# Weight loads that cast on the way, a changed order of GpSimd's early work, fewer loads per pair, and a last tile in halves

## Chip, cores, metric

The kernel runs on one core of a Trainium2 chip. The metric is the device time of one execution in microseconds. One execution was also recorded by the hardware profiler. Engines are named as in the profile: PE (TensorE matmul), PEld (its weight load), DVE (VectorE), ACT (ScalarE), POOL (GpSimd), SP (SyncE, which here only issues DMAs).

## What is computed

Attention with a sliding window and a few "sink" keys, followed by a two-layer network with a gate:

```python
# q, k, v: (4, 8, 768, 64) float32; n_sink = 4, window = 128
scores = matmul(q, k^T) / sqrt(64)
keep = (key position < 4) | (0 <= query position - key position < 128)
a = softmax(where(keep, scores, -1e9))
attn = matmul(a, v)                          # (4, 8, 768, 64)
x = attn.transpose(0, 2, 1, 3).reshape(3072, 512)
h = x @ w_in                                 # w_in: 512 x 2048
g = h * sigmoid(beta * h)
out = g @ w_out                              # w_out: 2048 x 512, out float32
```

## The kernel before, in words

**Tiling.** Two heads that lie side by side make a pair, and half a sequence (384 tokens) of a pair is a *unit* `n`: 32 units, of which four in a row (`4T` to `4T + 3`) give one tile `T` of 384 tokens by 512 channels. There are 8 tiles. `place(n)` gives a unit's batch, pair, half and buffer. A unit goes through these steps:

1. `load` (L372): q, k and v come by DMA as float32 into `q_stage`, `k_stage`, `v_stage`. Units 0 to 11 come half by half, units from 16 on for both halves of a pair at once, one DMA for each head of q, k and v, so six DMAs a pair.
2. `cast` (L417): POOL makes bf16 of q, k (into `qk16`, three buffers) and v (into `v_aug`).
3. Transposes: units 0 to 11 by PE (`transpose_in`, L447), later ones by a transposing DMA on SP's queue (L432).
4. Scores on PE (L487, L521), exponentials on ACT (L493, L528), masks on DVE (L502, L537: a product of two bf16 tiles), the product with v on PE (`attend`, L571), for the second half of a sequence with the sink keys too (`v_sink`, L560), then the normalisation on DVE (L581) and the way back into `xT` (L598, or a transposing DMA, L590).

**The network.** For each tile 16 blocks of hidden channels: `hidden` (L618, four 128x384 matmuls each), the tanh on ACT (L626), the gate on DVE (L639), and `project` (L646, three blocks of 128 tokens, 16 matmuls of 512 columns each), whose result ACT or DVE scales by 0.5 into `out_sb` (L654, L658), from where SP's queue stores it (L661).

**Weights.** Both weight matrices come in eight pieces of 0.5 MB each: 0 to 7 are `w_in`, 8 to 15 are `w_out`. `load_w(i)` (L407) issues a plain DMA on SP's queue into one of eight float32 buffers `wst`, and `cast_w(i)` (L412) is a copy on POOL that makes bf16 of it. `hidden` reads `w_in`: pieces 0 and 1 from block 0 on, 2 and 3 from block 4 on, 4 to 7 from block 8 on.

**Order.** The program is a list of operations with what they read and write. `Prog.order` (L140) plays them through with estimated durations and fixes from it, before the kernel runs, in which order each engine gets its instructions; at each step the operation that can start first is taken, the earlier in the list on a tie. For DMAs it holds one time, `dma_free`, at which all DMAs together are done with what was issued. `Prog.emit` then puts in the waits on semaphores. So a changed estimate or a new dependence can change the order on each engine.

The main list: constants; the loads of units 0 to 3 (v of units 0 and 1 on ACT's queue, the rest on SP's), weight pieces 0 to 3, units 4 to 7, weight pieces 4 to 7; units 0 to 3 through all their steps (`enter`, then scores, masks, `attend`), the POOL casts of pieces 0 to 3 and two small POOL DMAs for `v_sink` (L689) in `enter(1)`; then a loop over steps `s`, where step `s` runs one block of `hidden`, and units 4 to 31 are worked into it by the table `FIRST`. At step `FIRST[5] + 2 = -2` pieces 4 to 7 are cast and the loads of pieces 8 to 15 and of units 8 to 15 are listed; at step 2 pieces 8 to 15 are cast; at step 16 POOL copies the masks into `mask_all` (L767, L771: six copies), which units from 12 on use. From step 32 on (`S_P0`) `project` runs beside `hidden`, with `w_out`; after the last gate only `project` is left.

The list order is not the order in time: an operation without open dependences can be taken before earlier listed ones that wait. The chain of `mask_all` copies is an example: listed at step 16, they run on POOL at 5.64 us.

## Time and profile before

| | us |
|---|---|
| median of three runs (lowest, highest) | 240.41 (239.73, 241.25) |
| the profiled execution, whole | 241.05 |
| its span from first to last instruction | 239.3 |
| POOL's 64 casts of q and k, and 32 of v (L425, L428) | 36.4 and 17.1 busy |
| POOL's 16 weight casts (L414), mean of one | 1.04 |
| POOL's two `v_sink` DMA issues (L689), first at 4.28 | 0.62 and 0.76 |
| DVE's masks of units 0 to 11 (L502), 24 | 0.55 to 1.20 each |
| `project`'s matmuls (L646) | 98.5 busy |
| `hidden`'s matmuls (L618), both kinds of bank | 80.1 and 20.2 busy |
| issue to landing, weight loads of `w_in`, median | 6.8 |
| issue to landing, output stores (256 KB), median | 2.7; the last ones 2.0 |
| last PE matmul ends | 236.13 |
| last copy to `out_sb` (L654) | 236.21 to 236.81 |

How to read it: busy time counts an engine's instructions without its waits. "DMA share" is the mean busy share of the core's 16 DMA engines; overlapping packets can bring it over 1. The granted TensorE clock is 1.00 throughout. POOL's last cast of q and k begins at 149.5 us.

### The profile page before, as it was taken

What the parts mean: (1) busy time and instruction counts of PE and PEld (TensorE: products, weight loads), DVE (VectorE), ACT (ScalarE), POOL (GpSimd) and SP (SyncE); (2) the same over time, 40 slices, a digit from 0 to 9 for tenths busy, and PEclk for the clock granted to TensorE, in tenths of its full rate; (3) what the DMA queues carried; (4) which work ended last, traced back from release to release, by engine and by line L of the source; (5) the groups of instructions that cost most, each with busy time, mean ns of one, the idle gap of its engine ahead of it and who ended that gap; (6) DMA issues with size and microseconds to landing.
All of it is one profiled execution on the core that took longest, in us unless ns stands there. A gap on an engine that the chain in (4) does not pass through costs nothing.

```text
span 239.3 us, 4359 instructions
## 1 busy us (share of the span) xinstructions
PE 217.9 (91%) x1677; PEld 118.2 (49%) x1677; DVE 137.7 (58%) x262; ACT 147.7 (62%) x254; POOL 73.3 (31%) x134
## 2 busy tenths in 40 slices
PE   0567769799999999999999999999999999999994
PEld 0244435455545555554555555555555555555441
DVE  4066499859974565653676537664666656434300
ACT  2477487559852756765877667658767865554411
POOL 7989568529251133232223337000000000000000
PEclk9999999999999999999999999999999999999999
DMA  7999999899799999999999976512201022111022
GB/s 176 260 374 280 334 377 294 221 284 251 169 227 207 209 183 276 231 164 216 225 167 237 195 148 152 126 28 60 63 16 47 16 60 63 44 44 44 5 85 88
DMA packets 96084, 39.76 MB, mean 166 GB/s; under 512 B 82736, under 2 KB 88896, under 8 KB 96064
## 3 DMA queue, kind: packets, MB, share of 16 engines
q1 hardware_dynamic: 93888, 39.07, 71.0%
q10 hardware_dynamic: 1632, 0.40, 0.8%
q8 instruction: 13, 0.21, 0.4%
q0 software_dynamic: 544, 0.02, 0.2%
q14 instruction: 7, 0.06, 0.1%
HBM read 27.30 MB, written 6.29 MB: 140 GB/s over the span
## 4 chain that ended last, share of the span: by engine, by line
PE 81%; DVE 11%; ACT 4%; POOL 2%; issue 1%; ACTq 0%
PE acc L646 34%; PE h_ps L618 28%; PE s_ps L571 5%; DVE E L502 5%; PE acc L618 4%; PE s_ps L521 4%; ACT E L493 2%; DVE g L639 2%; DVE qkT L454 1%; PE h_ps L646 1%; PE s_ps L487 1%; PE s_ps L560 1%; DVE v_sink L335 1%; PE s_ps L469 1%; DVE o_norm L581 1%
## 5 line engine op out<-in xcount | busy, mean ns | idle before, releaser
L646 PE MATMUL acc<-w_out,g 128*128 128x512 bf16 x368 | 98.5, 380 | 0.0
L626 ACT ACTIVATE th<-h_ps,beta_half 128x384 f32<-128x384 f32 x104 | 59.3, 582 | 39.0 <-PE h_ps L618 37.6
L618 PE MATMUL h_ps<-xT,w_in 128*128 128x384 bf16 x416 | 80.1, 326 | 0.2 <-DVE g L639 0.2
L639 DVE SCALAR_TENSOR_TENSOR g<-th,h_ps 128x384 bf16<-128x384 f32 x104 | 56.3, 552 | 33.3 <-ACT th L626 31.9
L618 PEld LDWEIGHTS h_ps<-xT,w_in 128*128 128x128 bf16 x416 | 39.6, 98 | 30.9 <-DVE g L639 1.7
L646 PEld LDWEIGHTS acc<-w_out,g 128*128 128x128 bf16 x368 | 34.4, 98 | 33.4 <-issue 3.0
L537 DVE TENSOR_TENSOR E<-E,mask_all 128x1536 bf16<-128x1536 bf16 x20 | 19.7, 984 | 26.4 <-ACT E L528 26.4
L528 ACT ACTIVATE E<-s_ps 128x1536 bf16<-128x1536 f32 x20 | 29.0, 1449 | 7.5 <-PE s_ps L521 7.1
L425 POOL CAST qk<-q_stage 128x384 bf16<-128x384 f32 x32 | 18.8, 588 | 34.2 <-DMA qkT<-qk 17.9
L428 POOL CAST v_aug<-v_stage 128x384 bf16<-128x384 f32 x32 | 17.1, 546 | 36.8 <-PE s_ps L571 35.9
L571 PE MATMUL s_ps<-v_aug,E 128*128 128x65 bf16 x384 | 21.1, 199 | 3.2 <-DVE E L502 3.0
L571 PEld LDWEIGHTS s_ps<-v_aug,E 128*128 128x128 bf16 x384 | 18.1, 101 | 9.0 <-DVE E L502 4.1
L618 PE MATMUL acc<-xT,w_in 128*128 128x384 bf16 x96 | 20.2, 341 | 1.6 <-DVE g L639 1.3
L654 ACT ACTIVATE out_sb<-acc 128x512 f32<-128x512 f32 x23 | 13.6, 597 | 11.3 <-PE acc L646 10.8
L581 DVE TENSOR_TENSOR o_norm<-s_ps,rden 128x384 bf16<-128x384 f32 x32 | 17.8, 558 | 1.8
L626 ACT ACTIVATE th<-acc,beta_half 128x384 f32<-128x384 f32 x24 | 13.8, 585 | 7.9 <-PE acc L618 7.4
L425 POOL CAST qk<-k_stage 128x384 bf16<-128x384 f32 x32 | 17.6, 550 | 0.1
L493 ACT ACTIVATE E<-s_ps 128x768 bf16<-128x768 f32 x16 | 13.0, 812 | 4.9 <-PE s_ps L487 4.7
L639 DVE SCALAR_TENSOR_TENSOR g<-th,acc 128x384 bf16<-128x384 f32 x24 | 13.0, 548 | 2.8 <-ACT th L626 2.7
L447 PE MATMUL s_ps<-ident,qk 128*128 128x128 bf16 x60 | 6.3, 246 | 8.8 <-POOL qk L425 8.3
L502 DVE TENSOR_TENSOR E<-E,mask_b 128x768 bf16<-128x768 bf16 x16 | 13.5, 847 | 1.2 <-ACT E L493 0.9
L618 PEld LDWEIGHTS acc<-xT,w_in 128*128 128x128 bf16 x96 | 8.4, 102 | 8.0 <-DVE g L639 3.5
(58 smaller groups left out, 147.4 us busy)
## 6 DMA issues: line engine op xcount, KB each, us to landing
out_dram<-out_sb SPq DMA_DIRECT2D x24, 256.0 KB, 2.7
q_stage<-in_q_dram SPq DMA_DIRECT2D x28, 192.0 KB, 4.3
k_stage<-in_k_dram SPq DMA_DIRECT2D x28, 192.0 KB, 4.9
wst<-in_moe_w_in_dram SPq DMA_DIRECT2D x8, 512.0 KB, 6.8
wst<-in_moe_w_out_dram SPq DMA_DIRECT2D x8, 512.0 KB, 7.6
v_stage<-in_v_dram SPq DMA_DIRECT2D x16, 192.0 KB, 4.0
v_stage<-in_v_dram SPq DMA_DIRECT2D x28, 96.0 KB, 5.0
q_stage<-in_q_dram SPq DMA_DIRECT2D x8, 96.0 KB, 4.1
```

The lines of the kernel that those rows point to most:

```text
L425: op("gp", lambda e, x=x, name=name: e.tensor_copy(qk16[z][:, x, :, :, :], view(name)), r=[(name + "_stage", pb, half, hh) for hh in range ...
L428: op("gp", lambda e: e.tensor_copy(v_aug[pb][:, 3 * half:3 * half + 3, :, 0:D], view("v")), r=[("v_stage", pb, half, hh) for hh in range(2 ...
L493: op("act", lambda e: e.activation(E[n % 2][:, c, :, 0:at], bank[:, 0:2, 0:at], AF.Exp, bias=0.0, scale=SCALE), x=[f"{name}0", f"{name}1"] ...
L502: op("dve", lambda e: e.tensor_tensor(E[n % 2][:, c, :, 0:w], E[n % 2][:, c, :, 0:w], m[:, first:first + w].unsqueeze(1).to_broadcast([128 ...
L528: op("act", lambda e: e.activation(E[z][:, :, :, :].rearrange("p c h x -> p c (h x)"), s_ps[:, :, :].rearrange("p (h b) x -> p h (b x)", h ...
L537: op("dve", lambda e: e.tensor_tensor(both, both, mask_all[:, half, :].unsqueeze(1).to_broadcast([128, 2, 768]), ALU.mult), r=[("E", z, 0) ...
L571: last=(x == len(kbs) - 1): e.matmul(av_ps[:, at + hh * D1:at + hh * D1 + D1], E[z][:, c, h2, col:col + 128], v_aug[pb][:, kb, hh, :], sta ...
L581: op("dve", lambda e: e.tensor_tensor(o_norm[o][:, :, :, :].rearrange("p m h d -> p (m h) d"), src[:, :, 0:D], rden[z][:, :].unsqueeze(2). ...
L618: op("pe", lambda e: e.matmul(bank, w_in16[:, c, m * 128:(m + 1) * 128], xT[:, c, T * TT:(T + 1) * TT], start=(c == 0), stop=(c == 3)), r= ...
L626: op("act", lambda e: e.activation(th[i % 3][:, :], bank, AF.Tanh, bias=0.0, scale=beta_half[:, m:m + 1]), x=[name], r=["beta"], w=[("th", ...
L639: op("dve", lambda e: e.scalar_tensor_tensor(g[T % 2][:, m, :], th[i % 3][:, :], 1.0, bank, ALU.add, ALU.mult), r=[("th", i % 3)], x=[name ...
L646: op("pe", lambda e: e.matmul(bank, g[T % 2][:, m, t * 128:(t + 1) * 128], w_out16[:, m, :], start=(m == 0), stop=(m == NM - 1)), r=[("g", ...
```

## The change

- **Weights**: `wst`, `w_piece` and `cast_w` go. `load_w` is now a DMA issued by POOL that reads float32 and writes bf16 straight into `w_in16` or `w_out16`. Each has a new kind of dependence, `after`: it waits until the cast of a given unit's v is done. Pieces 0 and 1 wait for unit 2, pieces 2 and 3 for unit 3, 4 and 5 for unit 4, 6 and 7 for unit 5, 8 to 11 for unit 6, 12 to 15 for unit 7.
- **POOL's early work**: the six copies to `mask_all` wait for the cast of unit 7; the two DMAs for `v_sink` wait for that of unit 4.
- **Loads**: units 8 to 11 wait for the cast of unit 5; they and units 12 to 15 are listed without weight pieces between them. From unit 16 on, q, k and v of a pair are one DMA each, for both heads and both halves: three DMAs for six.
- **The planner's picture of DMAs**: one time per issuing queue, with the rate shared between a queue and the one that is busy longest.
- **The last 128 tokens**: `project` for them is done in two halves of 256 columns, one after the other, into the two banks of `h_ps`. The first is scaled by DVE and stored by SP's queue, the second by ACT and stored by ACT's queue.

```diff
@@ -100,7 +101,8 @@
 
         return Together()
 
-    def op(self, eng, fn, r=(), w=(), x=(), dma=None, busy=100.0, lag=None, behind=None):
+    def op(self, eng, fn, r=(), w=(), x=(), dma=None, busy=100.0, lag=None, behind=None,
+           after=()):
         if self.group is not None and self.group.eng == eng:
             node = self.group
         else:
@@ -116,7 +118,7 @@
             if not same or (raw and eng != "pe"):
                 events.append(ev)
 
-        for t in r:
+        for t in (*r, *after):
             dep(self.writer.get(t), True)
         for t in (*w, *x):
             dep(self.writer.get(t), False)
@@ -148,7 +150,7 @@
         head = dict.fromkeys(self.ENGINES, 0)
         can = {e: [n for n in left[e] if n.open == 0] for e in self.ENGINES}
         placed = []
-        dma_free = self.FIRST_DMA
+        ring = dict.fromkeys(self.ENGINES, self.FIRST_DMA)
 
         def best(e):
             q = left[e]
@@ -171,8 +173,11 @@
                 n.done = start + n.busy + n.lag
             else:
 
-                dma_free = max(dma_free, start + n.busy) + n.lag
-                n.done = dma_free + 2000.0
+                at = max(ring[e], start + n.busy)
+                other = max(t for q, t in ring.items() if q != e)
+                shared = max(0.0, other - at)
+                ring[e] = at + (2 * n.lag if 2 * n.lag <= shared else n.lag + shared / 2)
+                n.done = ring[e] + 2000.0
             n.place = start
             can[e].remove(n)
             placed.append(n)
@@ -280,7 +285,6 @@
     xT = sb("xT", (128, 4, NTOK), BF16)
     w_in16 = sb("w_in16", (128, 4, DF), BF16)
     w_out16 = sb("w_out16", (128, NM, NOUT), BF16)
-    wst = [sb(f"wst{i}", (128, 1024), F32) for i in range(NW)]
     beta_stage = sb("beta_stage", (16, 128), F32)
     beta_half = sb("beta_half", (128, NM), F32)
     ones = sb("ones", (128, 256), BF16)
@@ -369,50 +373,50 @@
 
         return n // 8, n % 4, n // 4 % 2, n % 4
 
-    def load(n, v_queue="sp"):
+    def load(n, v_queue="sp", after=()):
         b, hp, half, pb = place(n)
         t0 = half * TT
         if n < XBAR:
             for name, src in (("q", q), ("k", k)):
                 s = src[b, 2 * hp:2 * hp + 2, t0:t0 + TT, :].rearrange("h (p c) d -> p h (c d)", c=3)
                 d = stage[name][pb][:, :, 3 * half:3 * half + 3, :].rearrange("p h c d -> p h (c d)")
-                op("sp", lambda e, d=d, s=s: e.dma_start(d, s),
+                op("sp", lambda e, d=d, s=s: e.dma_start(d, s), after=after,
                    w=[(name + "_stage", pb, half, 0), (name + "_stage", pb, half, 1)],
                    dma=f"{name}{pb}_{half}", **transfer(2 * TT * D * 4, 329))
-        halves = (0, 1) if n >= WHOLE else (half,)
-        first, size = (0, 6) if n >= WHOLE else (3 * half, 3)
         for name, src in (("q", q), ("k", k), ("v", v)):
+            if n >= WHOLE:
+                s = src[b, 2 * hp:2 * hp + 2, :, :].rearrange("h (c p) d -> p (h c) d", p=128)
+                d = stage[name][pb][:, :, :, :].rearrange("p h c d -> p (h c) d")
+                op("sp", lambda e, d=d, s=s: e.dma_start(d, s), after=after,
+                   w=[(name + "_stage", pb, x, hh) for x in range(2) for hh in range(2)],
+                   dma=f"{name}{pb}_0", **transfer(2 * S * D * 4, 220))
+                continue
             if name != "v" and n < XBAR:
                 continue
             for hh in range(2):
-                s = src[b, 2 * hp + hh, 128 * first:128 * (first + size), :].rearrange(
-                    "(c p) d -> p c d", p=128)
+                s = src[b, 2 * hp + hh, t0:t0 + TT, :].rearrange("(c p) d -> p c d", p=128)
                 op(v_queue, lambda e, hh=hh, s=s, name=name: e.dma_start(
-                    stage[name][pb][:, hh, first:first + size, :], s),
-                   w=[(name + "_stage", pb, x, hh) for x in halves],
-                   dma=f"{name}{pb}_{half}{hh}", **transfer(size * 128 * D * 4, 220))
+                    stage[name][pb][:, hh, 3 * half:3 * half + 3, :], s), after=after,
+                   w=[(name + "_stage", pb, half, hh)],
+                   dma=f"{name}{pb}_{half}{hh}", **transfer(TT * D * 4, 220))
 
     w_in_src = moe_w_in.rearrange("(c p) f -> p c f", p=128)
     w_out_src = moe_w_out.rearrange("(m p) n -> p m n", p=128)
 
-    def w_piece(i):
-        z = i % NW
+    def load_w(i, behind):
+
         if i < NW:
-            c, n = 2 * (z % 2), 512 * (z // 2)
-            view = wst[z][:, :].rearrange("p (c f) -> p c f", c=2)
-            return view, w_in_src[:, c:c + 2, n:n + 512], w_in16[:, c:c + 2, n:n + 512]
-        view = wst[z][:, :].rearrange("p (m n) -> p m n", m=2)
-        return view, w_out_src[:, 2 * z:2 * z + 2, :], w_out16[:, 2 * z:2 * z + 2, :]
-
-    def load_w(i):
-        view, src, _ = w_piece(i)
-        op("sp", lambda e: e.dma_start(view, src), w=[("wst", i % NW)], dma=f"w{i % NW}",
-           **transfer(1 << 19, 389))
-
-    def cast_w(i):
-        view, _, dst = w_piece(i)
-        op("gp", lambda e: e.tensor_copy(dst, view), r=[("wst", i % NW)],
-           w=[("w_in" if i < NW else "w_out", i % NW)], busy=985.0, lag=100.0)
+            c, n = 2 * (i % 2), 512 * (i // 2)
+            src, dst = w_in_src[:, c:c + 2, n:n + 512], w_in16[:, c:c + 2, n:n + 512]
+        else:
+            m = 2 * (i - NW)
+            src, dst = w_out_src[:, m:m + 2, :], w_out16[:, m:m + 2, :]
+        op("gp", lambda e: e.dma_start(dst, src), after=cast_of(behind),
+           w=[("w_in" if i < NW else "w_out", i % NW)], dma=f"w{i}", busy=710.0,
+           lag=(1 << 19) / 350.0)
+
+    def cast_of(n):
+        return [("v_aug", place(n)[3], place(n)[2])]
 
     def cast(n):
         _, _, half, pb = place(n)
@@ -642,24 +646,26 @@
 
     n_out = [0]
 
-    def project(T, t, m, bank, name, eng="act"):
-        op("pe", lambda e: e.matmul(bank, g[T % 2][:, m, t * 128:(t + 1) * 128],
-                                    w_out16[:, m, :], start=(m == 0), stop=(m == NM - 1)),
-           r=[("g", T % 2, m), ("w_out", m // 2)], w=[name], **pe(NOUT))
+    def project(T, t, m, bank, name, eng="act", cols=slice(0, NOUT), queue="sp"):
+        width = cols.stop - cols.start
+        op("pe", lambda e: e.matmul(bank[:, 0:width], g[T % 2][:, m, t * 128:(t + 1) * 128],
+                                    w_out16[:, m, cols], start=(m == 0), stop=(m == NM - 1)),
+           r=[("g", T % 2, m), ("w_out", m // 2)], w=[name], **pe(width))
         if m == NM - 1:
             z = n_out[0] % 4
             n_out[0] += 1
 
             if eng == "act":
-                op("act", lambda e: e.activation(out_sb[z][:, :], bank, AF.Copy, bias=0.0,
-                                                 scale=0.5),
-                   x=[name], w=[("out_sb", z)], **act(NOUT))
+                op("act", lambda e: e.activation(out_sb[z][:, 0:width], bank[:, 0:width], AF.Copy,
+                                                 bias=0.0, scale=0.5),
+                   x=[name], w=[("out_sb", z)], **act(width))
             else:
-                op("dve", lambda e: e.tensor_scalar(out_sb[z][:, :], bank, 0.5, None, ALU.mult),
-                   x=[name], w=[("out_sb", z)], **dve(600.0))
+                op("dve", lambda e: e.tensor_scalar(out_sb[z][:, 0:width], bank[:, 0:width], 0.5,
+                                                    None, ALU.mult),
+                   x=[name], w=[("out_sb", z)], **dve(1.17 * width))
             row = T * TT + t * 128
-            op("sp", lambda e: e.dma_start(out[row:row + 128, :], out_sb[z][:, :]),
-               r=[("out_sb", z)], dma=f"o{z}", **transfer(128 * NOUT * 4, 389))
+            op(queue, lambda e: e.dma_start(out[row:row + 128, cols], out_sb[z][:, 0:width]),
+               r=[("out_sb", z)], dma=f"o{z}", **transfer(128 * width * 4, 389))
 
 
     constants()
@@ -667,12 +673,8 @@
         load(n, "act" if n < 2 else "sp")
     op("act", lambda e: e.dma_start(beta_stage[:, :], moe_beta.rearrange("(m p) -> m p", p=128)),
        w=["beta_stage"], dma="beta")
-    for i in range(4):
-        load_w(i)
     for n in range(4, 8):
         load(n)
-    for i in range(4, 8):
-        load_w(i)
     cast(0)
     cast(1)
 
@@ -680,14 +682,16 @@
         transpose_in(n, *((tr_ps, "tr") if n % 2 == 0 else (acc[0], "acc0")), "act")
         if n + 2 < 6:
             cast(n + 2)
-        if n == 1:
-            for i in range(4):
-                cast_w(i)
+        if n < 2:
+            load_w(2 * n, n + 2)
+            load_w(2 * n + 1, n + 2)
+        if n == 3:
             for hh in range(2):
                 rows = slice(HEAD1 * hh, HEAD1 * hh + NSINK)
                 s = v[:, :, 0:NSINK, :].rearrange("b (g h) s d -> s h (b g) d", h=2)[:, hh]
                 op("gp", lambda e, hh=hh, rows=rows, s=s: e.dma_start(v_sink[rows, :, hh, 0:D], s),
-                   w=[("v_sink", hh)], r=["v_sink"], dma=f"s{hh}")
+                   w=[("v_sink", hh)], r=["v_sink"], after=cast_of(4), dma=f"s{hh}", busy=650.0,
+                   lag=700.0)
 
     for n in range(4):
         enter(n)
@@ -747,40 +751,28 @@
             cast(n)
             if n >= XBAR and n % 8 >= 4 and n + 4 < NU:
                 load(n + 4)
+        if s == FIRST[4]:
+            for x in range(4, 8):
+                load_w(x, 4 if x < 6 else 5)
         if s == FIRST[5] + 2:
-            for x in range(4, 8):
-                cast_w(x)
-            for x in (8, 9, 10, 11):
-                load_w(x)
-            load(8)
-            load_w(12)
-            load_w(13)
-            load(9)
-            load_w(14)
-            load_w(15)
-            for n in range(10, 16):
-                load(n)
+            for n in range(8, 16):
+                load(n, after=cast_of(5) if n < 12 else ())
         if s == NM:
 
             first = {0: (mask_a[:, :], MASK_A), 1: (mask_b[:, 128:512], MASK_B)}
             for half in range(2):
                 op("gp", lambda e, half=half: e.tensor_copy(mask_all[:, half, 0:TT], first[half][0]),
-                   r=first[half][1], w=[("mask_all", half, 0)], busy=300.0)
+                   r=first[half][1], after=cast_of(7), w=[("mask_all", half, 0)], busy=300.0)
                 for x, n in ((0, 1), (1, 2)):
                     at = TT + 128 * x
                     op("gp", lambda e, half=half, n=n, at=at: e.tensor_copy(
                         mask_all[:, half, at:at + 128 * n], mask_b[:, 0:128 * n]),
-                       r=MASK_B, w=[("mask_all", half, 1)], busy=200.0)
+                       r=MASK_B, after=cast_of(7), w=[("mask_all", half, 1)], busy=200.0)
         if s == FIRST[7] + 1:
-
-            for x in (8, 9, 10, 11):
-                cast_w(x)
+            for x in range(8, 16):
+                load_w(x, 6 if x < 12 else 7)
             cast(8)
-            cast_w(12)
-            cast_w(13)
             cast(9)
-            cast_w(14)
-            cast_w(15)
         if S_P0 <= s < S_PIPE:
 
             for t, (bank, name, eng) in enumerate(
@@ -791,7 +783,14 @@
             T = (s - S_PIPE) // NM + 1
             for x in range(3 * (s % NM), 3 * (s % NM) + 3):
                 a = (3 * T + x // NM + 1) % 2
-                project(T, x // NM, x % NM, acc[a][:, :], f"acc{a}")
+                if (T, x // NM) != (NT - 1, 2):
+                    project(T, x // NM, x % NM, acc[a][:, :], f"acc{a}")
+        if s == S_END + NM - 1:
+
+            for c in range(2):
+                for m in range(NM):
+                    project(NT - 1, 2, m, h_ps[:, c, :], f"h{c}", "dve" if c == 0 else "act",
+                            slice(256 * c, 256 * c + 256), "sp" if c == 0 else "act")
         if i is not None:
             gate(i)
         for fn in later:
```

## The prediction

> **What bounds the kernel now.** I read the page first, then the windows (busy time by stretch), the chain of waits in order of time, what each engine waited for, and the DMA landings of single issues. The page gives the engines' totals:
>
> ```profile
> PE 217.9 (91%) x1677; PEld 118.2 (49%) x1677; DVE 137.7 (58%) x262; ACT 147.7 (62%) x254; POOL 73.3 (31%) x134
> DMA  7999999899799999999999976512201022111022
> ```
>
> TensorE is idle for 239.3 - 217.9 = 21.4 us. The windows show where (columns: window, length, busy PE, PEld, DVE, ACT, POOL, clock, DMA share, GB/s):
>
> ```profile
> 0.00:6.00 6.00, 0.00 (x0) 0.00 (x0) 2.51 (x9) 1.49 (x2) 4.39 (x17) 1.00 0.71 176
> 6.00:12.00 6.00, 3.01 (x21) 1.55 (x21) 0.50 (x1) 2.54 (x5) 6.00 (x16) 1.00 1.22 261
> 12.00:18.00 6.00, 3.89 (x42) 2.92 (x42) 4.09 (x7) 4.51 (x10) 4.91 (x6) 1.00 1.06 372
> 24.00:30.00 6.00, 4.78 (x31) 2.64 (x30) 2.64 (x5) 2.51 (x5) 3.43 (x8) 1.00 1.06 336
> 60.00:66.00 6.00, 6.00 (x54) 3.44 (x51) 5.82 (x13) 5.22 (x12) 1.59 (x4) 1.00 0.75 170
> 225.00:239.30 14.30, 11.12 (x52) 4.85 (x50) 0.57 (x2) 2.97 (x5) 0.00 (x0) 1.00 0.20 73
> ```
>
> All idle time lies before 60 us and in the last 3.1 us. From 60 to 236 us PE is full at clock 1.00 and waits for nobody, four 128x384 matmuls taking 0.65 us and three 128x512 ones 0.65. That stage can neither gain nor lose unless data comes late. So the change is worth what it moves in the first 60 us and in the tail. The chain says what sets the start (start, duration, what):
>
> ```profile
> 4.28 0.96 POOL v_sink L689 x2
> ...
> 5.64 0.52 POOL mask_all L767
> 6.16 0.57 POOL mask_all L771 x2
> 6.73 0.44 POOL mask_all L767
> 7.17 0.58 POOL mask_all L771 x2
> 7.75 0.39 POOL qk L425
> 8.14 0.02 issue
> 8.16 0.50 POOL qk L425
> ```
>
> POOL, not the DMA, delays the first casts: they stand behind two DMA issues and six mask copies. What PE waited for agrees:
>
> ```profile
> PE s_ps L447 <- POOL qk L425: 8.3, 1, 8.3
> ```
>
> **The change, part by part**, against the profiled execution's 241.05 us (span 239.3 plus 1.75 around it). It lies 0.64 over the median of the runs, 240.41, and inside their range.
>
> *Head.* v_sink's DMAs (4.28 to 5.65) and the mask copies (5.64 to 7.75) leave the front of POOL, whose constants end at 3.45. Then data decides: q of unit 0 is issued at 0.81 and lands 3.1 later, at 3.9; k is issued at 1.32 and lands 3.6 later, at 4.9. Its k cast starts at 4.92 instead of 8.16: 3.24 earlier. Can units 1 to 3 follow? k of unit 1 lands at 2.33 + 5.0 = 7.3 (cast now 9.52), of unit 2 at 3.35 + 5.5 = 8.9 (now 10.88), of unit 3 at 5.44 + 6.7 = 12.1 (now 12.24). Unit 3's cannot come earlier, but its transposes run at 15.8 now, so 12.6 is possible after a cast of 0.50. I take -3.2; bounds -3.8 (q's whole lead, 7.71 - 3.9) and -1.0 (units 2 and 3 set the pace).
>
> *First weights.* Pieces 0 and 1 are now issued by POOL behind cast 2, whose v lands at 9.8: cast to 10.3, issues at 10.3 and 11.0 by the 0.68 us that a v_sink issue took (616 and 757 ns, DVE idle). The slowest of the first four weight loads needed 8.3 us, so 11.0 + 8.3 = 19.3. The first hidden matmuls stand at 23.97 in the chain, 20.7 after the shift. Cost 0, hidden under units 0 to 3, with 1.4 us to spare; beyond that each us of delay is a us. Behind the issues in POOL's order wait cast 3 (k lands at 12.1, after them) and then cast 4, which today stands behind four weight casts (14.41 to 19.55), so is no later.
>
> *DMA supply.* The DMA share is above 1 in nearly every window to 40 us, so bytes are not free. Today's single SP queue brings units 4 to 7 before weight pieces 4 to 7. Afterwards pieces 4 to 7 follow casts 4 and 5 on POOL's queue and meet units 6 and 7. They are 2.1 MB, 5.6 us at the best rate of these windows (372 GB/s). Unit 6's v is cast at 24.75, right on its landing (idle 0.24), its transposes run at 31.59: 6.3 us of room, 3.1 after the shift. All weights ahead of it costs 5.6 - 3.1 = +2.5; half ahead, nothing. I take +0.7. Loads 8 to 11 gain a wait for cast 5 on SP; behind them stand only later loads, and cast 8 is not used before step 22, some 55 us. The last pieces follow casts 6 and 7 (28.8 now) and are needed at 65.43: hidden.
>
> *v_sink* is issued after cast 4 (ends 21.60 now) and landed 5.8 to 6.7 after issue: 21.6 + 1.4 + 6.2 = 29.2 if cast 4 doesn't move and both issues go first, while its first reader, at 32.09 now, moves to 28.9. I take +0.2 (cast 4 a little earlier); bounds 0 and +3.1 (two weight pieces of 1.4 us, 0.5 MB at 372 GB/s, ahead of it on its queue).
>
> *VectorE beside POOL.* The 16 weight casts of 1.04 us go; 16 issues (by the row above 11 us) come. The masks L502 take 0.55 alone and up to 1.19 beside a POOL cast. Four places of the chain show it (1.09, 0.99, 1.10 and 1.60 for two):
>
> ```profile
> 31.66 1.09 DVE E L502
> ...
> 33.62 0.99 DVE E L502
> ...
> 36.58 1.10 DVE E L502
> ...
> 40.49 1.60 DVE E L502 x2
> ```
>
> Over 0.55 each that is 2.0 us. Gain -2.0 if issues leave VectorE alone; the moved mask copies (2.1 us of POOL, behind cast 7, in that same stretch) and issues that block it like a cast could make it +1.0. No row has an issue beside busy VectorE. I take the middle, nearer to the gain: -1.0.
>
> One rule weighs in here, in sentences that the sum does without. The Trainium skill, page "SBUF — State Buffer", section "Who interferes with whom", says that an instruction with two SBUF inputs on VectorE contends with GpSimd's SBUF reads only; an issue reads no tensor, so by the rule this term is -2.0. Its section "SBUF: two separate sides" speaks against the change: descriptors of a GpSimd DMA starve while VectorE holds the shared ports, a 620 ns DMA becoming 3100 ns. An estimate from that page: two issues 2.4 us longer bring piece 1 to 24.1 us, 3.4 past need, and the sum to near zero.
>
> *Tail.* The last projection (128 tokens) becomes 16 + 16 matmuls of 256 columns: 32 x 107 ns is 16 x 213, if the 98 ns weight loads stay under them as in L646's 51 matmuls in 11.02 us. Left after the last one now: copy 0.60, a 256 KB DMA of 2.0 us. A copy of half the columns, between 0.20 (one column, L340) and 0.60, is 0.40; 128 KB less at 372 GB/s saves 0.35; the ACT queue issue costs what SP's did (0.45 to 0.5). I take -0.5; bounds -0.6 and +0.3.
>
> *Three DMAs a pair.* 8 units load whole pairs, 48 issues become 24 of the same bytes, some 12 us of SP's time. Transposing DMAs behind them on SP go sooner, but PE waits for nothing after 65 us: 0. All engines' orders are re-planned; I put 1 us either way into the range for it.
>
> Sum: -3.2 + 0 + 0.7 + 0.2 - 1.0 - 0.5 = -3.8, 237.25 by the profiled execution, 236.6 by the median.
>
> **Rivals.** *Given back by the DMA*: the front moves by 3.2, but units 3 to 7 come no earlier than now, as the full DMA row to 40 us suggests; what the masks save is then waited for too, and the tail's -0.5 is left: 239.9. Against it: 3 us of room at unit 6.
> *First weights late (slower)*: at the first hidden matmuls, PE stands until piece 1 has landed. If casting DMAs issued by POOL need twice the slowest row, 16.6 us, it lands at 27.6, 3.6 us past today's 23.97; less the tail 0.5, +3.1: 243.5. It decides from a landing past 24.5 us, that is 13.5 after the issue at 11.0. For it: the DMAs are full then, and no row has a casting DMA. Against: 2 KB packets of the weights raised the rate to 372 GB/s, and only half the bytes are written.
> *Nothing to gain at the front*, since data is late anyway, falls by the landings above for unit 0.
>
> **How the numbers follow.** Forecast 0.62 (236.6), given back 0.20 (239.9), weights late 0.18 (243.5). A time of 1% either way, 2.4 us, is about what a measurement of this kernel tells from no change: under 238.0 is faster, over 242.8 slower. So faster 0.62, same 0.20, slower 0.18. The forecast's own range: head at -3.8, masks at -2.0, supply at 0 and 1 us of re-planning give 236.6 - 3.3 = 233.3; supply at its bound gives 236.6 + 1.8 = 238.4. The range reaches on through the given-back case with re-planning against it (+1.0) and the tail at its bound (+0.8): 241.7. Left out is mostly the late case, under 2 in 10.
>
> **What would show it.** First POOL cast at about 4 us and first transposes by 5 (head); no long PE wait at the first L618 (weights), at L560 (v_sink) or at the transposes of units 6 and 7 (supply); masks of 0.55 rather than 1.1 between 28 and 40 us (contention); the full stretch of PE starting about 3.3 us earlier with 176 us unchanged; 2.5 us or less from PE's last matmul to the end (tail). Wrong it would be if weight DMAs land over 13 us after issue, if POOL's issues take several us, or if PE waits after 60 us.

## The result and the profile after

The changed kernel takes 243.68 us (median of four runs, 242.29 to 245.2). The kernel before takes 240.66 us (four runs, 239.73 to 241.25). The ratio is 1.0136, 95% interval 1.009 to 1.0181, so the change makes the kernel about 3 us slower. The forecast was 236.6, with a range of 233.3 to 241.7. The profiled execution of the changed kernel took 245.2 us, with a span of 243.5, against 241.05 and 239.3 before. Ratios here and below leave out runs that fell into a slower state, while each time given is the median of all runs; e7_all and e11_nqk were profiled in such a run and stand in no table.

First the page: the engines' totals, and the rows of granted clock and DMA share (40 slices of 6.1 us).

```profile
PE 219.4 (90%) x1670; PEld 120.1 (49%) x1693; DVE 134.4 (55%) x263; ACT 147.9 (61%) x254; POOL 69.3 (28%) x134
...
PEclk9999999979999799999999999999999999999999
DMA  6999999988999999999997455720211112100122
```

TensorE's idle time is 243.5 - 219.4 = 24.1 us, against 21.4 before. So the 3 us saved at the front came back as idle time elsewhere, and two slices of the row `PEclk`, the TensorE clock that was granted in tenths of full speed, show a 7 that was not there. The windows tell where (columns: window, length, busy PE, PEld, DVE, ACT, POOL, clock, DMA share, GB/s):

```profile
0.00:6.00 6.00, 1.00 (x6) 0.47 (x6) 2.51 (x9) 1.54 (x3) 4.12 (x17) 1.00 0.68 164
6.00:12.00 6.00, 3.25 (x30) 1.99 (x30) 1.19 (x2) 3.91 (x7) 3.77 (x7) 1.00 1.13 290
24.00:30.00 6.00, 4.97 (x57) 2.86 (x57) 4.16 (x7) 5.13 (x10) 5.18 (x10) 1.00 1.24 213
48.00:54.00 6.00, 3.55 (x17) 1.62 (x16) 2.85 (x6) 2.78 (x6) 4.03 (x10) 0.76 0.91 232
60.00:66.00 6.00, 5.85 (x51) 3.17 (x51) 5.82 (x13) 4.92 (x10) 2.47 (x6) 1.00 0.86 195
78.00:84.00 6.00, 3.33 (x25) 1.99 (x25) 1.99 (x4) 2.11 (x4) 1.98 (x4) 0.82 1.25 183
84.00:90.00 6.00, 4.92 (x28) 2.27 (x28) 3.23 (x6) 3.08 (x4) 0.73 (x2) 0.89 1.32 226
```

The same windows of the kernel before, for the three that matter now:

```profile
48.00:54.00 6.00, 5.68 (x43) 3.33 (x42) 3.53 (x8) 3.20 (x7) 1.49 (x4) 1.00 1.02 289
78.00:84.00 6.00, 6.00 (x51) 3.27 (x50) 3.33 (x6) 4.74 (x7) 0.97 (x2) 1.00 1.20 208
84.00:90.00 6.00, 6.00 (x47) 3.30 (x47) 3.75 (x7) 3.48 (x7) 1.87 (x4) 1.00 1.37 176
```

The front is ahead, as forecast. Then, against the kernel before, PE loses 2.1 us of busy time at 48 to 54 us and 3.75 us at 78 to 90 us, and in both places the clock falls. The waits of PE name what it stood for (total us, times, longest):

```profile
PE s_ps L451 <- POOL qk L429: 8.5, 5, 4.4
PE s_ps L473 <- DMA qkT<-qk: 3.8, 2, 2.7
```

Of the first line, 4.4 us is the start of the program (8.3 before) and 2.1 us is new, at 48.5 us: PE's transposes wait for casts, which wait for data. The second line is all new: PE waits for transposing DMAs, which bring units 12 and up. (L473 is the matmul of a unit with the sink keys, the first of a second-half unit.)

To follow the lead through the run, count DVE's gate instructions (L639 before, L643 after). There are 128 and they are the same work in both kernels. The table gives the start of one, and for the other kernels of this study the difference to it (negative is ahead). From the 33rd gate on the columns also move with the work that the planner puts between two gates: in the changed kernel the difference goes from +4.8 at the 64th to -1.6 at the 68th without a stall. So they are read together with PE's waits.

| kernel (profiled execution) | 1st | 9th | 17th | 25th | 32nd | 33rd | 128th |
|---|---|---|---|---|---|---|---|
| before, us | 28.5 | 44.3 | 53.8 | 61.0 | 66.1 | 81.9 | 225.8 |
| changed | -3.1 | -5.1 | -5.0 | -1.2 | -1.2 | +2.2 | +4.6 |
| e10_nofront | -0.3 | -0.9 | -0.8 | -1.3 | -1.2 | +5.5 | +5.8 |
| e1_front | -3.7 | -8.2 | -0.1 | -1.6 | +0.5 | +0.9 | +1.1 |
| e9_planfront | -1.7 | -1.2 | -1.2 | -1.3 | -1.3 | -1.3 | -1.3 |
| e13_fronttail | -2.2 | -2.9 | -2.9 | -2.8 | -2.8 | -2.8 | -3.0 |
| e3_six | -3.2 | -5.3 | -5.2 | -5.0 | -5.0 | +1.1 | +2.9 |
| e4_order | -3.0 | -5.1 | -5.0 | -5.5 | -5.4 | +3.0 | +4.7 |
| e5_wlate | -3.5 | -5.6 | -5.5 | -5.9 | -5.8 | -2.0 | +3.0 |
| e6_defer | -3.5 | -5.5 | -5.4 | -5.3 | -5.3 | -3.8 | -1.4 |
| e12_nqkonly | -2.8 | -5.0 | -4.9 | -4.8 | -4.5 | -4.8 | +11.4 |
| e15_lesswout | -3.9 | -6.0 | -5.9 | -6.1 | -6.1 | -6.0 | -0.3 |
| e16_deferless | -3.4 | -5.5 | -5.4 | -5.5 | -5.5 | -5.6 | -5.7 |

In the changed kernel a lead of 5.0 us stands at 53.8. The first stall takes 3.8 of it, and the second stretch turns -1.2 into +4.6; the tail gives back about 0.5, which leaves the 4.2 us by which the spans differ. The chain of waits shows the second stretch (start, duration, what):

```profile
66.45 5.20 DMA qkT<-qk
...
72.25 1.74 POOL qk L429 x3
73.99 1.60 SPq L390
75.63 5.12 DMA qkT<-qk
80.80 0.34 PE s_ps L473
...
84.00 0.42 SPq L390
84.47 5.19 DMA qkT<-qk
89.70 0.34 PE s_ps L473
```

The second and third transposing DMAs in it, of units 13 and 14, release PE directly. (The step from POOL's casts to SP's load at 73.99 is inferred by the profile; in the program that load waits for unit 13's q cast alone, which had ended at 66.9.) SP's own issues say why they come so late (start, duration of the issue, line, operation, tile; a whole-pair load is 384 KB):

```profile
63.22 1.30 SPq L390 DMA_DIRECT2D v_stage<-in_v_dram  x2
64.56 1.84 SPq L390 DMA_DIRECT2D q_stage<-in_q_dram  x1
66.45 2.64 SPq L436 DMA_TRANSPOSE qkT<-qk  x1
69.15 0.56 SPq L390 DMA_DIRECT2D k_stage<-in_k_dram  x1
69.76 4.11 SPq L390 DMA_DIRECT2D v_stage<-in_v_dram  x2
73.91 1.68 SPq L390 DMA_DIRECT2D q_stage<-in_q_dram  x1
75.63 2.61 SPq L436 DMA_TRANSPOSE qkT<-qk  x1
```

And in the kernel before (here a load is 192 KB):

```profile
64.96 1.31 SPq L432 DMA_TRANSPOSE qkT<-qk  x1
66.32 1.18 SPq L390 DMA_DIRECT2D k_stage<-in_k_dram  x2
67.55 1.13 SPq L390 DMA_DIRECT2D v_stage<-in_v_dram  x2
68.72 1.02 SPq L390 DMA_DIRECT2D q_stage<-in_q_dram  x1
69.78 1.54 SPq L432 DMA_TRANSPOSE qkT<-qk  x1
```

SP is never idle here; it issues in order, and all casts that these loads wait for had ended by 67. Unit 13's casts run on POOL at 66.06 and 66.89, so its data is ready at 67.4, but its transposing DMA goes out 8.2 us later, behind four loads of units 16 to 19 that nobody needs yet: 4 x 384 KB = 1.5 MB, where there were 5 x 192 KB = 1.0 MB. Before, its casts ended at 65.4 and 4.4 us passed to its issue. So of the 5.85 us by which this DMA goes later, 2.0 are later casts and 3.8 are spent on SP. The planner's new order also puts units 13, 15, 14 one after the other where it had 13, 14, 15, so that unit 14 goes 5.9 us later than before as well (84.47 against 78.59).

### The profile page after: what moved, and what is told of

It is laid out like the page before. It is cut to its first block, busy times and chain, and to the rows that moved or that the text cites. A ratio compares the mean times of both kernels' runs of the same rounds, so it can differ in the third digit from the quotient of the medians.

```text
span 243.5 us, 4324 instructions
## 1 busy us (share of the span) xinstructions
PE 219.4 (90%) x1670; PEld 120.1 (49%) x1693; DVE 134.4 (55%) x263; ACT 147.9 (61%) x254; POOL 69.3 (28%) x134
## 4 chain that ended last, share of the span: by engine, by line
PE 59%; SPq 20%; DMA 15%; issue 2%; POOL 2%; ACT 1%; DVE 0%; POOLq 0%; ACTq 0%
PE acc L651 25%; PE h_ps L622 24%; SPq L383 10%; DMA qkT<-qk 9%; SPq L398 8%; DMA v_stage<-in_v_dram 6%; PE s_ps L575 3%; PE s_ps L525 3%; PE h_ps L651 2%; PE s_ps L564 1%; PE s_ps L473 1%; POOL v_aug L432 1%; POOL qk L429 1%; SPq L390 1%; ACT E L532 1%
## 5 line engine op out<-in xcount | busy, mean ns | idle before, releaser
L651 PE MATMUL acc<-w_out,g 128*128 128x512 bf16 x330 | 92.0, 382 | 1.2 <-issue 0.3
L622 PE MATMUL h_ps<-xT,w_in 128*128 128x384 bf16 x416 | 82.8, 328 | 0.1
L643 DVE SCALAR_TENSOR_TENSOR g<-th,h_ps 128x384 bf16<-128x384 f32 x104 | 56.8, 550 | 40.3 <-ACT th L630 39.6
L622 PEld LDWEIGHTS h_ps<-xT,w_in 128*128 128x128 bf16 x416 | 40.3, 98 | 34.5 <-issue 1.3
L651 PEld LDWEIGHTS acc<-w_out,g 128*128 128x128 bf16 x352 | 32.0, 98 | 29.6 <-issue 3.6
L429 POOL CAST qk<-q_stage 128x384 bf16<-128x384 f32 x32 | 19.3, 602 | 55.7 <-DMA qkT<-qk 31.4
L532 ACT ACTIVATE E<-s_ps 128x1536 bf16<-128x1536 f32 x20 | 28.9, 1444 | 4.4 <-PE s_ps L525 4.1
L622 PE MATMUL acc<-xT,w_in 128*128 128x384 bf16 x96 | 21.3, 356 | 1.5 <-DVE g L643 1.0
L575 PE MATMUL s_ps<-v_aug,E 128*128 128x65 bf16 x384 | 20.5, 201 | 0.2 <-DVE E L541 0.2
L643 DVE SCALAR_TENSOR_TENSOR g<-th,acc 128x384 bf16<-128x384 f32 x24 | 13.0, 549 | 3.5 <-ACT th L630 3.3
L583 DVE RECIPROCAL rden<-s_ps 128x6 f32<-128x6 f32 x32 | 6.2, 193 | 10.4 <-PE s_ps L575 10.2
```

Of the source, the lines that this page charges most:

```text
L429: op("gp", lambda e, x=x, name=name: e.tensor_copy(qk16[z][:, x, :, :, :], view(name)), r=[(name + "_stage", pb, half, hh) for hh in range ...
L532: op("act", lambda e: e.activation(E[z][:, :, :, :].rearrange("p c h x -> p c (h x)"), s_ps[:, :, :].rearrange("p (h b) x -> p h (b x)", h ...
L575: last=(x == len(kbs) - 1): e.matmul(av_ps[:, at + hh * D1:at + hh * D1 + D1], E[z][:, c, h2, col:col + 128], v_aug[pb][:, kb, hh, :], sta ...
L622: op("pe", lambda e: e.matmul(bank, w_in16[:, c, m * 128:(m + 1) * 128], xT[:, c, T * TT:(T + 1) * TT], start=(c == 0), stop=(c == 3)), r= ...
L643: op("dve", lambda e: e.scalar_tensor_tensor(g[T % 2][:, m, :], th[i % 3][:, :], 1.0, bank, ALU.add, ALU.mult), r=[("th", i % 3)], x=[name ...
L651: op("pe", lambda e: e.matmul(bank[:, 0:width], g[T % 2][:, m, t * 128:(t + 1) * 128], w_out16[:, m, cols], start=(m == 0), stop=(m == NM ...
```

## The experiments

**Theories**, formed from these traces. A: the loads of units 8 and 9 come too late, since units 12 to 15 stand ahead of them on SP. B: the DMAs have too many bytes to bring before 70 us; whatever comes first, something else is late. C: three large DMAs for a pair hold back what follows more than six small ones. D: the transposing DMAs of units 12 and up stand on SP behind early loads of units 16 and up. A fifth, that re-planning of the engines' orders decides, came up with e1_front. Each ratio below is against the kernel before on the same chip (240.05 to 240.68 us).

**e1_front**: the kernel before, with the front of the change alone (`after` and `cast_of` are put in as in the change).

```diff
...
-        if n == 1:
+        if n == 3:
...
-                   w=[("v_sink", hh)], r=["v_sink"], dma=f"s{hh}")
+                   w=[("v_sink", hh)], r=["v_sink"], after=cast_of(4), dma=f"s{hh}", busy=650.0,
+                   lag=700.0)
...
-                   r=first[half][1], w=[("mask_all", half, 0)], busy=300.0)
+                   r=first[half][1], after=cast_of(7), w=[("mask_all", half, 0)], busy=300.0)
```

> The kernel before with one part alone: the mask copies wait for cast 7, v_sink's DMAs for cast 4; weights still come in plain DMAs on SP's queue with POOL casts, old planner, six DMAs a pair, whole last tile. Theory A (order of the DMAs: the changed kernel loses after 44 us because w_out and unit 12 are brought ahead of units 8 and 9): here the old SP order stays, so the front's lead (first transposes at 4.4 instead of 8.3, first hidden matmuls about 3 us earlier) is kept to the end: about 237.5. Theory B (the DMAs as a whole are full until some 66 us, so that PE's later stage cannot start earlier whatever comes first): the lead is given back before 80 us: 239.5 to 241. Seen by the first project matmul: 62.5 us by A, 65 by B (65.4 now).

243.96 us, ratio 1.0148 (1.0089 to 1.0208): slower, though PE begins as early as in the changed kernel. The table shows -8.2 at the 9th gate and -0.1 at the 17th. v_sink's first reader, which stands at 32.09 before, stands at 42.16 here, and PE then waits in more places for DVE's gates. So this run is mixed with a new order of the work, and says nothing on the front itself; the next run, which differs from it by the way of planning alone, shows that re-planning is worth several us and not the 1 us of the prediction.

**e9_planfront**: the same with the change's way of planning DMAs (a time for each queue), and still with plain weight loads and six DMAs a pair.

```diff
...
-        dma_free = self.FIRST_DMA
+        ring = dict.fromkeys(self.ENGINES, self.FIRST_DMA)
...
```

> The kernel before with the front alone (mask copies behind cast 7, v_sink behind cast 4) and the new planner's picture of DMAs, weights still plain DMAs on SP with POOL casts. With the old picture the planner had put the first reader of v_sink at 42 us and the time rose to 244. If that order was the cause there, v_sink's reader comes back to about 29 us and the first project matmul to 62 or 63; by theory D or B the rest is then lost at units 12 and 13: 239 to 242; without such a loss 237.5.

238.89 us, ratio 0.991 (0.9873 to 0.9947): faster than both kernels. Its lead of 1.3 us is the same from the 9th gate to the last; no wait for a transposing DMA appears (issued at 64.63 and 69.40, as before). So with plain weight loads the front gives 1.7 us at the first gate and 1.3 from the 9th on, not the 3.2 of the prediction.

**e13_fronttail**: e9_planfront with the last 128 tokens in halves, as in the change's last hunks.

> The kernel before with the front of the change (mask copies and v_sink's DMAs later), the change's way of planning the DMAs and the last tile in halves; weights are loaded plain and cast by POOL, q, k and v of a pair come in six DMAs, as before. Without the halves it was 238.9 us. If the tail is worth what the profile of the changed kernel shows (2.7 us from PE's last matmul to the end against 3.2), 238.4; if nothing, 238.9. If the last 32 matmuls of half width cost PE more than the shorter store saves, 239.3 or more.

239.1 us, ratio 0.989 (0.9834 to 0.9947). Between 0.991 and 0.989 the intervals do not tell, so 0.5 us of the tail is neither shown nor refuted by the times.

**e10_nofront**: the changed kernel with its front undone (the reverse of e1_front's edit).

> The changed kernel with the front undone: mask copies and v_sink's DMAs at the front of POOL again, all else changed. If the front's 3.2 us were kept to the end, this is 3.2 us slower than the changed kernel: 246.9. Theories B and D: units 12 and 13 come when the DMAs let them, the front's lead only becomes waiting there, and the time is that of the changed kernel or less: 242 to 244.5.

245.93 us, ratio 1.0214 (1.0151 to 1.0277). By the ratios the front is worth 0.8%, some 1.9 us, inside the changed kernel, though the two intervals overlap. PE's wait is there without the front, 4.9 us at 78.2. e9_planfront has the new planning, and e13_fronttail the new tail too, without such a loss, so what is left for the loss is the weights' part of the change with the loads that were re-ordered for it, and the three DMAs a pair. Unit 13's casts end only at 75.33 here, and its transposing DMA goes out 3.1 us later, so most of this delay lies ahead of SP.

**e3_six**: the changed kernel with six DMAs for a pair.

```diff
-                s = src[b, 2 * hp:2 * hp + 2, :, :].rearrange("h (c p) d -> p (h c) d", p=128)
+                for hh in range(2):
+                    s = src[b, 2 * hp + hh, :, :].rearrange("(c p) d -> p c d", p=128)
...
```

> The changed kernel with one part undone: six DMAs a pair from unit 16 on instead of three. Theory C (whole-pair DMAs of 384 KB on SP hold up the transposing DMAs behind them, 5.2 us to landing instead of 3.6, and so make PE's wait of 2.7 us for qkT at 78 to 81 us): that wait goes and the time falls by 2 to 4 us, to about 240.5. Theories A and B: the transposes are late because the casts of units 12 and 13 are, the same bytes lie ahead of them, and the time stays at 243 to 244 with PE still waiting at units 12 to 13.

244.59 us, ratio 1.0179 (1.0116 to 1.0242). The wait for a transposing DMA is 4.4 us at 74.4, so six small loads do not cure it, and theory C does not explain the time. That the size of a load does nothing is not shown: unit 13's transposing DMA goes out 3.7 us after its casts and lands in 3.3 us here, against 8.2 and 5.1 in the changed kernel. But here the planner puts unit 15's casts ahead of unit 13's on POOL, and these end at 71.64 instead of 67.39.

**e4_order** and **e5_wlate**: the changed kernel with units 12 to 15 behind units 8 to 11, and with w_out behind the casts of units 8 and 9.

```diff
@@ e4_order
-                load(n, after=cast_of(5) if n < 12 else ())
+                load(n, after=cast_of(5))
@@ e5_wlate
-            for x in range(8, 16):
-                load_w(x, 6 if x < 12 else 7)
-            cast(8)
-            cast(9)
+            for n in (8, 9):
+                cast(n)
+                for x in range(4 * n - 24, 4 * n - 20):
+                    load_w(x, n)
```

> The changed kernel, with units 12 to 15 also waiting for cast 5, so that they are listed and issued behind units 8 to 11 on SP. Theory A: unit 8, which now stands behind unit 12's 0.6 MB (22.6 to 28.3 us on SP), is issued some 5 us sooner, its q cast moves from 43.95 to about 40, and PE's waits for POOL casts at 48 to 51.5 us (4.4 and 2 us) shrink by 2 to 4 us: 240 to 242. Theory B: units 8 and 9 come sooner, but unit 12 and 13 later, and the total stays within 1 us of 243.5.

> The changed kernel, with the w_out pieces issued behind casts 8 and 9 instead of 6 and 7. Theory A: 4.2 MB less stand in competition with units 8 to 11 between 30 and 45 us; unit 8's casts move from 44 to 49.5 us to about 38 to 42, PE's waits at 48 to 51.5 us go, w_out still lands before 60 us: 239 to 241. Theory B: the bytes only change places, the wait appears later (at w_out or at units 12 and 13): 242.5 to 244.

244.73 us (1.0182, 1.0133 to 1.023) and 244.57 us (1.0184, 1.013 to 1.0237). Both do what they say: the stall at 48 us is gone and the lead at the 32nd gate is 5.4 and 5.8 us instead of 1.2. And both lose it all in the next stretch, where PE waits 6.7 and 6.4 us for transposing DMAs (2.5, 3.9 and 0.3; 1.5, 2.1 and 2.8). Unit 13's stands 8.2 and 8.7 us on SP after its casts. Theory A describes a real stall whose removal alone is worth nothing: what was gained there is waited for later.

**e6_defer**: the changed kernel with each load from unit 16 on listed two units later, and behind that unit's cast.

```diff
-            if n >= XBAR and n % 8 >= 4 and n + 4 < NU:
-                load(n + 4)
+            if n - 2 >= XBAR and (n - 2) % 8 >= 4 and n + 2 < NU:
+                load(n + 2, after=cast_of(n))
```

> The changed kernel, with the loads of units from 16 on listed two units later and waiting for the cast that stands there (load 16 behind cast 14, and so on). Theory D (the transposing DMAs of units 12 and 13, issued at 66.5 and 75.6 us and landing 5.2 us later, stand on SP's queue behind whole-pair loads of units 16 to 18 that nobody needs yet; PE then waits at 78 to 81 us and runs at a lower granted clock after it): both go out as soon as their casts are done, PE's wait of 3.8 us for qkT goes, the clock stays at 1.00 past 60 us: 238 to 240.5. Theory B (the DMAs are full with what must come first): the transposes land no earlier than now, 242.5 to 244.

239.21 us, ratio 0.9961 (0.9926 to 0.9996): 4.2 us better than the changed kernel (1.0136 - 0.9961 = 1.75% of 240.65). Of the waits for transposing DMAs, 3.8 us in all, one is left, at 74.0:

```profile
PE s_ps L473 <- DMA qkT<-qk: 1.5, 1, 1.5
```

The edit has a second effect: in the new plan unit 8's loads go out from 25.39 instead of 28.32, and the stall at 48 us shrinks to 0.3. So the fair comparison is with e4_order, which has the same lead at the 32nd gate: 1.0182 - 0.9961 = 2.2%, 5.3 us. Theory D holds, but of a lead of 5.3 us at the 32nd gate only 1.4 is left at the end. Of the 3.9 us lost, the trace shows 3.1 as PE's waits: the 1.45 above, and 1.15 and 0.49 at 151 to 153, behind ACT, which waits 2.66 us for another transposing DMA. **e7_all** puts this edit together with those of e4_order and e5_wlate:

> The same with units 12 to 15 behind units 8 to 11 and w_out behind casts 8 and 9, so that the first project matmul comes at about 60 us, as it did with each of these alone (59.6 and 59.9). Theory D: this lead of 5.5 us over the kernel before (65.3) is kept, less a wait of 1 or 2 us: 235 to 238. Theory B: it is lost again at units 12 to 15, 241 to 244.

240.53 us, ratio 0.9985 (0.9946 to 1.0025): nothing on top of it, against an expected 235 to 238 or 241 to 244.

**e11_nqk** and **e12_nqkonly**: six buffers for cast units instead of three (`NQK = 6`), in e6_defer and in the changed kernel.

> The kernel with the late loads of units 16 and up (e6_defer, 239.2 us, which still loses some 4 us of its lead of 5.3 us after 60 us) with six buffers qk16 for cast units instead of three, so that the casts of units 13 to 15 do not wait until PE has transposed units 10 to 12. If those buffers hold the transposing DMA of unit 13 back (theory: buffers), it is issued by 65 us instead of 71, PE's wait of 1.45 us for it at 75 us goes, and the time is 235.5 to 238. If what is left of the loss is the DMAs' own supply (theory B), unit 13 still comes late, PE waits as before and the time stays at 239 to 240.

> The changed kernel (243.7 us) with six buffers qk16 instead of three and nothing else. If the three buffers alone keep the transposing DMAs of units 12 and 13 back, PE's wait of 3.8 us for them goes and the time is 239 to 240.5. If the whole-pair loads of units 16 and up that stand ahead of them on SP keep them back (theory D), the wait stays within 1 us of what it was and the time is 242.5 to 245.

241.32 us (1.0031, 1.0001 to 1.0061), 0.7% slower than e6_defer and outside both expectations, and 252.99 us (1.0497, 1.0447 to 1.0547): far worse than the changed kernel, which no theory had expected. The chain of e12_nqkonly tells how:

```profile
90.00 5.06 DMA qkT<-qk
95.08 0.20 ACT k_sink L464
95.31 0.19 ACT k_sink L464
95.51 0.59 ACT th L630
96.12 0.57 DVE g L643
96.73 1.46 PE h_ps L622 x4
```

Units 12 to 15 go out earlier or in time (60.67 to 80.67): unit 13's casts no longer wait for a buffer and end at 57.05, PE waits at most 0.34 us for these units, and the lead of 4.8 us still stands at the 33rd gate. So the buffers are part of what keeps unit 13 late in the changed kernel, with all its bytes in place. But unit 16's transposing DMA goes out only at 90.00, behind loads up to that of unit 24. This time it is ACT that waits, with the copy of unit 16's sink keys, and behind it in ACT's order stands a tanh that the network needs. PE loses 6.5 us at once. More buffers let casts run ahead, and each cast sets free a staging buffer, whose next load then gets onto SP ahead of a transposing DMA: unit 24's q load waits for unit 20's q cast, which ends at 81.0.

**e15_lesswout** and **e16_deferless**: the changed kernel and e6_defer with two of eight pieces of w_out loaded, so that each projection uses four blocks of w_out in turn and its sums are other ones. Open was then whether the rest is supply.

```diff
-            for x in range(8, 16):
-                load_w(x, 6 if x < 12 else 7)
+            for x in range(8, 10):
+                load_w(x, 6)
...
-                                    w_out16[:, m, cols], start=(m == 0), stop=(m == NM - 1)),
+                                    w_out16[:, m % 4, cols], start=(m == 0), stop=(m == NM - 1)),
...
```

> The changed kernel (243.7 us) with two of the eight pieces of w_out loaded: each projection uses the same four blocks of 128 hidden rows of w_out in turn, so its sums are other ones; PE's work and every wait but those for the six pieces are the same, and 3.1 MB less is read by 45 us, some 8 us of the DMAs at the 372 GB/s of the best window. If the bytes that the DMAs have to bring before 70 us are what makes units 8, 9 and 13 late (theory B), PE's waits at 48 and 78 us both go and the lead of 5 us lasts to the end: 235 to 237. If the order of the issues on SP alone does it (loads 8 to 11 behind 12 to 15, transposing DMAs behind the loads of units 16 and up), those waits stay at half their length or more, and the time is 240.5 to 243.5.

> The kernel with the late loads of units 16 and up (239.2 us) with the same six pieces of w_out left out. If supply is what still takes 4 us of its lead after 60 us, 235 to 237, the same as the kernel above; if the order of its casts and transposing DMAs takes it, the wait at 75 us stays and the time is 238 to 239.5.

241.69 us (1.0072, 1.0028 to 1.0116) and 235.75 us (0.98, 0.9728 to 0.9871). Supply alone does not save the changed kernel. Its lead of 6.0 us now lasts past the 33rd gate, and then goes in one piece, by a transposing DMA three units on. The chain of e15_lesswout:

```profile
77.45 4.25 DMA qkT<-qk
81.72 0.19 ACT k_sink L464
81.92 1.35 ACT E L532
83.27 0.14 issue
83.41 0.32 PE s_ps L473
```

Unit 16's transposing DMA goes out 2.7 us after its casts (74.76), behind that of unit 14 and a load. ACT waits for it, an exponential stands behind that on ACT, and PE stands for 4.0 us. With the late loads as well, that wait is gone. The window of e15_lesswout first (columns as above):

```profile
78.00:84.00 6.00, 1.82 (x10) 0.84 (x10) 0.71 (x1) 2.24 (x5) 3.78 (x8) 0.97 1.16 287
```

And of e16_deferless:

```profile
78.00:84.00 6.00, 5.95 (x51) 3.36 (x50) 3.51 (x7) 3.69 (x7) 1.92 (x4) 1.00 1.52 231
```

e16_deferless keeps its 5.5 us to the last gate. So both count, and the order of the loads first: the late loads alone give 1.75%, and 2.7% when the bytes are there in time; the bytes alone give 0.6%, with overlapping intervals, and 1.6% when the transposing DMAs do not stand behind later loads. The issue times and PE's need side by side (us; PE's need is the start of L469 or L473, the first matmul of the second-half units 13 and 14 that reads the sink keys):

| kernel | casts of 13 end | issue, unit 12 | 13 | 14 | 16 | PE at unit 13 | at unit 14 |
|---|---|---|---|---|---|---|---|
| before | 65.37 | 64.96 | 69.78 | 78.59 | 91.29 | 79.47 | 88.38 |
| changed | 67.39 | 66.45 | 75.63 | 84.47 | 87.86 | 80.80 | 89.70 |
| e3_six | 71.64 | 63.86 | 75.38 | 81.85 | 85.51 | 78.74 | 86.39 |
| e6_defer | 66.00 | 60.44 | 71.17 | 74.17 | 76.52 | 75.46 | 81.77 |
| e12_nqkonly | 57.05 | 60.67 | 66.63 | 74.25 | 90.00 | 74.47 | 80.47 |
| e15_lesswout | 66.19 | 58.80 | 68.74 | 74.06 | 77.45 | 73.23 | 83.41 |
| e16_deferless | 64.30 | 57.35 | 65.31 | 67.92 | 72.33 | 73.64 | 79.63 |

Before, a transposing DMA landed a median of 3.6 us after its issue, but unit 13's took longer (count, issue in ns, start; then issue to landing):

```profile
L432 SPq DMA_TRANSPOSE qkT<-qk x1: 1539/1539/1539, 69.8 to 69.8; - x1
...
DMA to landing us min/median/max: 5.6/5.6/5.6
```

So it was there at 75.40, 4.1 us before PE asked, and unit 14 at 82.71, 5.7 us before. That reserve is what the change used up. Unit 13's DMA goes 5.85 us later and lands in 5.12 us instead of 5.62, and PE asks at 78.13, where its wait begins, 1.34 us earlier: 5.85 - 0.50 + 1.34 - 4.07 = 2.6 us, the wait of 2.67.

## Why the prediction was wrong, step by step

*Head: right.* POOL's first cast starts at 3.88, PE's first transposes at 4.44 and the first gate 3.1 us earlier; -3.2 was forecast.

*First weights: right.* POOL's issues took 0.71 to 0.87 us each, and the first hidden matmuls start at 20.98 without a wait; 20.7 was forecast. The room was smaller than the 1.4 us put down: the slowest of the first four weight loads had needed 8.8 us (9.70 to 18.46), not 8.3, and piece 1 landed at 20.36. The last two pieces of w_out landed 13.7 and 14.7 us after their issue, past the 13 us named as a sign of being wrong, and nothing waited for them. *v_sink: right*: its reader starts at 28.99, forecast 28.9.

*VectorE beside POOL: right for the masks, their share of the time is not settled.* From the 1st to the 9th gate the lead grows from 3.1 to 5.1 us, and the masks of units 0 to 11 get shorter. Those with `mask_b` in the kernel before (count, then duration in ns: least, median, most):

```profile
L502 DVE TENSOR_TENSOR E<-E,mask_b x16: 559/852/1189, 12.6 to 73.2; 128x768 bf16<-128x768 bf16 x16
```

The same work in the changed kernel:

```profile
L506 DVE TENSOR_TENSOR E<-E,mask_b x16: 544/559/829, 9.5 to 71.9; 128x768 bf16<-128x768 bf16 x16
```

And in e10_nofront, which has the weights of the change and not its front:

```profile
L506 DVE TENSOR_TENSOR E<-E,mask_b x16: 544/552/559, 12.2 to 71.9; 128x768 bf16<-128x768 bf16 x16
```

A median of 852 ns became 559. The rule of the Trainium skill, page "SBUF — State Buffer", section "Who interferes with whom", is that a VectorE instruction with two SBUF inputs contends with a GpSimd instruction that reads SBUF; the shorter masks agree with it. By it the term was -2.0, where the sum took -1.0. The lead did grow by 2.0, but that this is owed to the masks alone is not shown: in e10_nofront they are as short, and the lead grows by 0.6 only. That page's other section, "SBUF: two separate sides", spoke of descriptors that starve while VectorE holds the shared ports in a two-port mode; the issues above, 0.71 to 0.87 us each, do not show it.

*DMA supply: this step failed first.* It weighed only weight pieces 4 to 7 against units 6 and 7, and for loads 8 to 11 it said that "behind them stand only later loads, and cast 8 is not used before step 22, some 55 us". But PE's order moved forward with the front: unit 8's transposes stood at 51.51 before and stand at 46.50 now, while SP issues unit 12's loads from 22.55 on and unit 8's only from 28.32. POOL waits 8.8 us for unit 8's q, and unit 9's transposes, due at 48.5, run at 50.6. Removing that stall won nothing (e4_order, e5_wlate), which shows that it was not the last word.

*Three DMAs a pair: this is the step that decides.* "Transposing DMAs behind them on SP go sooner, but PE waits for nothing after 65 us: 0." Both halves are wrong. They go later, unit 13's at 75.63 against 69.78, because its casts end 2.0 us later and because four loads of 384 KB, not five of 192 KB, stand ahead of it on SP; and that PE waits for nothing holds only as long as its reserve lasts, 4.1 us at unit 13. The reserve was never worked out, although a lead of 3.3 us (the sum without the tail) was forecast to run straight into it: it would have been just enough had the DMA landed when it did before. PE's waits for these DMAs come to 3.8 us where the term was 0, and the half clock after them is on top. e6_defer shows the price of the order of these issues: 4.2 us against the changed kernel, 5.3 against e4_order, with whatever else its plan moved. Undoing the three DMAs alone gains nothing (e3_six).

*Tail: as forecast by the profile.* From PE's last matmul to the end of the span it is 2.7 us instead of 3.2; the times do not resolve it.

*Re-planning: the term of the range that was mis-sized.* Put at 1 us either way, without a run or a row for it, it moved units 14 and 15 past each other, and by itself it separates e1_front from e9_planfront by 2.4% of the time.

The time came to lie at the figure of the rival "first weights late", 243.5, by chance and not by that mechanism: no PE wait for weights appears. What neither the forecast nor a rival had is a transfer that gets late in the full stretch, by order and not by bytes alone, though the prediction did name a PE wait after 60 us as a sign of being wrong.

Open: why e1_front is slower to the end, and how much of the 4 us that e6_defer still loses is owed to its order of units (12, 15, 13, 14) rather than to supply; the only kernels with the transposing DMAs in their old order and the weights cast by DMA, e11_nqk and e12_nqkonly, have six buffers as well. Each edit also let the planner re-order other work, so no run moves one DMA and nothing else.

## What to carry to other kernels

A lead won at the start is only kept if every later transfer has at least that much reserve: before counting it, take for each stage the landing time and the time at which the data is asked for, and write down the difference. A queue that issues in order delays a small urgent DMA by what is listed ahead of it, here by 8.2 us; prefetches for much later work belong behind it, and a free buffer is a reason to look at what will be issued early. When a stall vanishes and the time stays, look for the same lead being lost at the next transfer.

## What the hardware showed that was not expected

After some waits of PE the granted clock drops to 0.5 for 3.4 us, in the full stretch too. In the changed kernel it is 0.5 from 51.2 to 54.6 and from 81.9 to 85.3, after waits of 2.1 + 0.3 and 2.7 us; in e3_six once after 4.4, in e10_nofront once after 4.9, in e5_wlate once after 2.8, in e15_lesswout once after 4.0, in e12_nqkonly after 2.7, in e7_all after 2.9 and again after two waits of 1.4 and 0.5, and for 6.8 us around a wait of 3.9 in e4_order, 6.5 in e12_nqkonly and 3.2 in e11_nqk. Waits of 2.5 us earlier in e4_order, of 2.1 in e5_wlate, of 1.45 in e6_defer and 1.1 in the changed kernel were followed by none, and neither before nor e9_planfront nor e16_deferless has one before the last us. Eight 128x384 matmuls took 2.77 us at 51.5 in the changed kernel and 1.46 at 45.2. So by estimate 3.4 us do the work of 1.7, and where PE is full such a wait costs some 1.7 us more than it lasts. The Trainium skill, page "TensorE: Matmul & The Clock Gate", section "HAM oscillation — how this bites in real kernels", states the rule as no idle gaps of more than about 3.4 us; here gaps of 2.4 to 2.8 us were enough, though not each time, and once two of 1.9 together.

An issue on SP's queue is not of fixed cost. One load of v took 2.9 us to issue at 70.9 in the changed kernel, though the cast that it waits for had ended at 66.1; the DMA share was 1.33 from 66 to 72 us. One of half the size took 0.54 us at 67.6 before. The transposing DMAs of units 12, 13 and 14 took 2.6 us each (1.3 to 1.7 before). So what stands behind is delayed at the issue already; that a full queue is the reason was not tried by itself.
